# A sigmoid-attention and token-mixing kernel: every transpose in 64x64 tiles, PSUM as four pairs of banks, and a rewritten order

## The chip, the cores and the metric

The kernel runs on one core of a Trainium2 chip. The metric is the device time of one execution in microseconds (us), lower is better. The kernel before was timed three times: 203.85, 204.28 and 204.39 us, median 204.28 us.

Engine names in what follows are those of the profile: PE is TensorE's matmuls, PEld its weight loads, DVE is VectorE, ACT is ScalarE, POOL is GpSimd, SP is SyncE, which here only issues DMAs.

## The reference

Two stages, with batch B = 8, H = 12 heads, S = 448 tokens, head size 64, model size D = 768:

```python
scores = q @ k^T / sqrt(64) - log(S)          # per batch and head: 448 x 448
attn   = 1 / (1 + exp(-scores))               # a sigmoid, no softmax
x      = attn @ v, heads side by side         # (8, 448, 768)

wq, wk = x @ w_q, x @ w_k                     # (8, 448, 64) each
W_tok  = wq @ wk^T / sqrt(64)                 # token by token, per batch
mixed  = W_tok @ x
out    = max(mixed, 0) @ w_out                # (8, 448, 768), float32
```

Inputs and output are float32. Both kernels compute in bfloat16 with float32 accumulation.

## The kernel before, in words

Four heads of one batch are a **quad**; there are 24 quads, three to a batch. A quad's q, k and v arrive as one DMA each (`load1`, 448 KB), POOL casts them to bfloat16 (`cast1`), PE transposes q and k (`tr`), and DVE copies the transposes from PSUM to SBUF. For quads 16 to 22 (`TWICE`) q and k take another way: four DMAs load them in an overlapping layout (216 KB each, so 864 KB in place of 448 KB), POOL casts them into pairs, and DVE's own transpose (L154) does the work that PE does for the others.

The work is named by letters, and one string, `PLAN`, is the order written out by hand in which they are issued. PE runs its instructions in that order:

- `S` (`scores`): one seventh of a quad's scores, four 64x64-tile matmuls of 448 columns, one in each quarter of the array; then one ACT sigmoid of 128 x 896 into `at`. There are 168 of them, seven to each line of `PLAN`.
- `P` (`values`): one seventh of attn @ v, four 64x64-tile matmuls of 448 columns, accumulated over seven; after the seventh a DVE copy to `xt`.
- `q`, `k` (`tr`): seven transposes on the whole 128x128 array, then a DVE copy. `K` is a rest of the first quad's k.
- `x` (`tr_x`): eight 128x128 transposes of `xt`, DVE copy to `xn`.
- `W`, `N`, `U`, `M` (`mlp_wqk`, `mlp_wkn`, `mlp_tmp`, `mlp_mix`): the token mixing of one batch. `W` is a 128x128 matmul of 448 columns, `N` four 128x128 transposes, `U` eight 128x64-tile matmuls of 384 columns, `M` four 64x64-tile matmuls of 448 columns and a relu.
- `O` (`out_chunk`): a 128 x 384 piece of the output, six 128x128 matmuls of 384 columns, then a copy to SBUF and, for every second one, two DMAs to the output. In `U`, `M` and `O` a small letter puts the copy on ACT, a capital on DVE.

So PE works in three ways of splitting its array: 64x64 (`S`, `P`, `M`), 128x128 (`q`, `k`, `x`, `W`, `N`, `O`) and 128x64 (`U`).

PSUM has eight banks. Three pairs (`free2`) serve `S`, `P` and `M`; two single banks (`free1`) serve all other steps. A step takes the bank that has been free longest, so the order of release decides which reader a step waits for.

Loads are issued on SP in the order of the list `ORDER`, each as soon as its buffer is free (`pump_loads`); the casts run on POOL in the same order (`pump`). The last line of `PLAN` has no `S` left: its steps, with the last output pieces, are the tail, where copies are shared out between DVE and ACT and half of the stores are issued from ACT.

Of the kernel before, what the change touches and what calls it, by code (L numbers as in the profile page):

```python
# [16 lines left out]
def kernel(  # L17
# [36 lines left out]
    p_lb = pool("lb", 2)  # L54
# [10 lines left out]
    ps_f = pool("ps_f", 1, space=bass.MemoryType.PSUM)  # L65

    free2 = ["a", "b", "c"]
    free1 = ["d", "e"]

    def bank2(name):  # L70
        n = free2.pop(0)
        return n, ps_q.tile([P, 2, 512], F32, tag=n, name=name)

    def bank(shape, dtype, name):
        n = free1.pop(0)
        return n, ps_f.tile(shape, dtype, tag=n, name=name)
# [23 lines left out]


    TWICE = {'q': (16, 17, 18, 19, 20, 21, 22), 'k': (16, 17, 18, 19, 20, 21, 22)}

# [3 lines left out]
    def load1(n, nm, eng):  # L107
        u, j = quads[n]
        if n in TWICE.get(nm, ()):
            t = p_lb.tile([P, 2, 14 * HD], F32, tag=nm + "b32", name=nm + "b32")  # L110
            for g in range(2):
                src = SRC[nm][u, 4 * j + 2 * g : 4 * j + 2 * g + 2].rearrange(
                    "h (p r) d -> p h (r d)", r=14
                )
                for dh in range(2):
                    r0 = 64 * g + 32 * dh
                    eng.dma_start(  # L117
                        out=t[r0 : r0 + 32, :, 0 : 13 * HD + 32],
                        in_=src[:, :, 32 * dh : 32 * dh + 13 * HD + 32],
                    )  # L120
        else:
            t = p_ld.tile([P, 2, NI * HD], F32, tag=nm + "32", name=nm + "32")
            eng.dma_start(  # L123
                out=t,
                in_=SRC[nm][u, 4 * j : 4 * j + 4].rearrange(
                    "(g h) (p i) d -> (h p) g (i d)", g=2, i=NI
                ),
            )
        ld[nm, n] = t

    def cast1(n, nm, eng):
        if n in TWICE.get(nm, ()):
            t16 = p_c16.tile([P, 2, NI, 32, 2], BF16, tag=nm + "16", name=nm + "16")
            eng.tensor_copy(  # L134
                out=t16.rearrange("p h i d y -> p h y i d"),
                in_=ld.pop((nm, n)).rearrange("p h (y i d) -> p h y i d", y=2, d=HD)[..., 0:32],
            )
        else:
            p = p_v16 if nm == "v" else p_c16
            t16 = p.tile([P, NI, 2, HD], BF16, tag=nm + "16", name=nm + "16")  # L140
            eng.tensor_copy(  # L141
                out=t16.rearrange("p i b d -> p b i d"),
                in_=ld.pop((nm, n)).rearrange("p b (i d) -> p b i d", i=NI),
            )
        ld[nm + "16", n] = t16

    qk = {}

    def tr(n, nm):
        t16 = ld.pop((nm + "16", n))  # L150
        t = p_qk.tile([P, 2, NI, NP], BF16, tag=nm + "t", name=nm + "t")
        qk[nm, n] = t
        if n in TWICE.get(nm, ()):
            nc.vector.transpose(  # L154
                out=t.rearrange("p h i n -> p (h i n)").bitcast(F32),
                in_=t16.rearrange("p h i d y -> p (h i d y)").bitcast(F32),
            )
            return
        fb, ps = bank([P, NI, 2, NP], BF16, "pt" + nm)
        for i in range(NI):  # L160
            nc.tensor.transpose(  # L161
                ps[:, i].rearrange("p h n -> p (h n)"),
                t16[:, i].rearrange("p b d -> p (b d)"), ident16,
            )
        nc.vector.tensor_copy(out=t, in_=ps.rearrange("p i h n -> p h i n"))  # L165
        free1.append(fb)
# [3 lines left out]
    def scores(n, i):  # L170
        fb, sc = bank2("sc")
        for g in range(2):
            for h in range(2):
                nc.tensor.matmul(  # L174
                    sc[HALF[h], g, 0:S], qk["k", n][HALF[g], h, i, :],
                    qk["q", n][HALF[g], h].rearrange("p i n -> p (i n)"), start=True, stop=True,
                )
        at = p_at.tile([P, 2, S], BF16, tag="at", name="at")
        nc.scalar.activation(at, sc[:, :, 0:S], ACTF.Sigmoid, bias=bias_t, scale=attn_scale)  # L179
        free2.append(fb)  # L180
        ats[n, i] = at
# [3 lines left out]
    def values(n, i, tail):  # L185
        u, j = quads[n]
        if i == 0:
            pv[n] = bank2("pv")
        fb, ps = pv[n]
# [6 lines left out]
        if i == NI - 1:  # L196
# [5 lines left out]
            free2.append(fb)  # L202
# [3 lines left out]
    def tr_x(n, tail):  # L206
        u, j = quads[n]
        if j == 0:
            xns[u] = p_x.tile([P, 4, D], BF16, tag="xn", name="xn")
        fb, ps = bank([P, 4, 2, 2, HD], BF16, "px")  # L210
        for h in range(2):
            for m in range(4):
                nc.tensor.transpose(  # L213
                    ps[:, m, :, h], xt(u, j)[:, h, m * P : (m + 1) * P], ident16
                )
        for g in range(2) if tail else (slice(0, 2),):
            w = slice(2 * j * P, 2 * (j + 1) * P) if not tail else slice((2 * j + g) * P, (2 * j + g + 1) * P)
            COPY["s" if tail and g else "v"](  # L218
                out=xns[u][:, :, w],
                in_=ps[:, :, g].rearrange("p m h d -> p m (h d)")  # L220
                if tail else ps.rearrange("p m g h d -> p m (g h d)"),
            )
        free1.append(fb)
# [4 lines left out]
    def mlp_wqk(u, c, tail):  # L228
        if c == 0:
            pw[u] = bank([P, S], F32, "pw")  # L230
        fb, ps = pw[u]
# [3 lines left out]
        if c == NC - 1:  # L235
# [6 lines left out]
            free1.append(fb)  # L242

    def mlp_wkn(u):
        fb, ps = bank([P, 4, P], BF16, "pk")
        for m in range(4):
            nc.tensor.transpose(ps[:, m], wqks[u % 2][:, m * P : (m + 1) * P], ident16)
        wkn[u] = p_one.tile([P, 4, DH], BF16, tag="wkn", name="wkn")
        nc.vector.tensor_copy(out=wkn[u], in_=ps[:, :, 64:128])
        free1.append(fb)  # L250

    def mlp_tmp(u, act):
        tmps[u] = p_one.tile([P, NB], BF16, tag="tmp", name="tmp")
        fb, ps = bank([P, NB], F32, "pt")
# [7 lines left out]
        free1.append(fb)  # L262
# [7 lines left out]
    def mlp_mix(u, c, act, tail):  # L270
        if c == 0 and u % 2 == 0:
            mxs[u // 2] = [p_mx.tile([P, 2, 2, S], BF16, tag=f"mx{n}", name="mx") for n in range(NC // 2)]
        fb, ps = bank2("pm")
# [13 lines left out]
        free2.append(fb)  # L287
# [3 lines left out]

    def out_chunk(act, tail):
        w, m, nb = chunks.pop(0)
        if nb == 0:
# [3 lines left out]
        def block(ps, w0, w1):  # L298
            for c in range(NC):
# [14 lines left out]
        fb, ps = bank([P, NB], F32, "po")  # L314
        if tail and w == NU // 2 - 1 and not chunks:
            h = NB // 2
            block(ps[:, 0:h], NB, NB + h)
            nc.vector.tensor_copy(out=o[:, NB : NB + h], in_=ps[:, 0:h])
            fb2, ps2 = bank2("po")
            block(ps2[:, 0, 0:h], NB + h, D)  # L320
            nc.scalar.copy(out=o[:, NB + h :], in_=ps2[:, 0, 0:h])
            store(slice(NB, NB + h))
            store(slice(NB + h, D))
            return
        block(ps, nb * NB, (nb + 1) * NB)
        COPY["s" if act else "v"](out=o[:, nb * NB : (nb + 1) * NB], in_=ps)  # L326
        free1.append(fb)
# [39 lines left out]
    fb, ps = bank2("pwarm")  # L367
    for _ in range(32):
        nc.tensor.matmul(ps[:, 0, 0:P], zeros, zeros, start=True, stop=True)
    free2.append(fb)  # L370
    for t in xts:
        nc.vector.memset(t[:, :, S:], 0.0)
    for t in wqks:
# [4 lines left out]
        "v0 q1 k1 v1 k2 q2 q3 k3 q4 k4 v2 k5 k6 w0 k7 v3 "  # L378
        "w1 q5 q6 k8 v4 w2 q7 w3 v5 w4 k9 q8 v6 q9 w5 w6 "
        "v7 q10 k10 v8 v9 q11 k11 q12 v10 k12 v11 q13 k13 k14 q14 q15 "  # L380
        "v12 q16 k15 v13 v14 q17 k16 v15 k17 q18 k18 q19 v16 k19 v17 k20 "
        "k21 v18 v19 v20 v21 q20 q21 q22 v22 q23 k22 k23 v23 "
# [3 lines left out]
    BACK = {}  # L386
    for nm in "qkv":
        mine = {True: [], False: []}
        for n in range(N):
            kind = n in TWICE.get(nm, ())  # L390
            BACK[nm, n] = (kind, list(mine[kind]))
            mine[kind].append(n)

    def pump_loads():
        while len(loaded) < len(ORDER):
# [5 lines left out]
            else:  # L401
                kind, before = BACK[nm, n]
                back = 2 if kind else 3
                if len(before) >= back and (nm, before[-back]) not in cast:
# [35 lines left out]
    for nm in "qk":  # L440
        qk[nm, 0] = p_qk.tile([P, 2, NI, NP], BF16, tag=nm + "t", name=nm + "t")

    def tr_part(nm, t16, r, e, b=None):
        shape = [P, r.stop - r.start, 2, NP]
        fb, ps = (None, ps_q.tile(shape, BF16, tag=b, name="pt" + nm)) if b else bank(shape, BF16, "pt" + nm)
        for i in range(r.start, r.stop):
            nc.tensor.transpose(
                ps[:, i - r.start].rearrange("p h n -> p (h n)"),
                t16[:, i].rearrange("p b d -> p (b d)"), ident16,
            )  # L450
        COPY[e](out=qk[nm, 0][:, :, r], in_=ps.rearrange("p i h n -> p h i n"))  # L451
        if fb:
            free1.append(fb)
# [3 lines left out]
    tr_part("k", k016, KA, "v", free2[-1])  # L457
# [7 lines left out]
        "SSSKSPPSqPSkSPPP",  # L465
        "SSqPSkSqSPkSqSPPPP",
        "SkSPPSxSSkPPPPSxSk",
# [90 lines left out]
```

## Time and profile before

| what | value |
|---|---|
| median of 3 runs | 204.28 us (203.85 to 204.39) |
| the profiled execution | 204.95 us, of which the span of the program is 203.2 us |
| PE busy | 192.2 us (95%), 2388 matmuls |
| ACT busy | 171.2 us (84%) |
| DVE busy | 123.1 us (61%) |
| POOL busy | 80.3 us (40%) |
| read from HBM, written | 41.75 MB, 11.01 MB |
| TensorE clock granted, mean | 0.992 |
| first `S` matmul, last sigmoid's end, end of the span | 6.38, 177.69, 203.2 us |

A busy PE is not PE at its peak: a matmul's row lasts longer than the time after which the next one may start. Where one row of the chain of waits follows the other on PE without a gap, the rows' lengths are what a step costs. The profiled execution was 0.67 us above the median, and 1.75 us of it lies outside the span.

### The profile page before, as it was taken

The page shows a single profiled execution, that of the slowest core. Times are in us where ns is not written, and L with a number is a line of the kernel's source. Part 1 is how long each engine was busy: PE and PEld are TensorE (multiplying, and loading weights), DVE is VectorE, ACT ScalarE, POOL GpSimd, SP SyncE. Part 2 cuts the span into 40 slices and gives each one's busy share as a digit, 9 for nine tenths or more (in the row PEclk, how much of TensorE's full clock was granted, in tenths as well). Part 3 has the DMA queues.
Part 4 walks back from the last instruction along what each step waited for, and adds up shares of the span by engine and source line. Part 5 has one row for each costly group of instructions (what it writes and reads, how often), then busy time and mean ns, then how long its engine had stood idle before and what let it go on. Part 6 is the DMA issues. An engine that isn't in the chain of part 4 may idle for free.

```text
span 203.2 us, 5863 instructions
## 1 busy us (share of the span) xinstructions
PE 192.2 (95%) x2388; PEld 108.6 (53%) x2388; DVE 123.1 (61%) x196; ACT 171.2 (84%) x200; POOL 80.3 (40%) x95
## 2 busy tenths in 40 slices
PE   7669999999999999999999999999999899999991
PEld 7335545545556566555656555545455455555561
DVE  2226655866498567668777776858777654471230
ACT  4796999999989999889999999898998959974511
POOL 1577688676416624217642442511632600000000
PEclk9996999999999999999999999999999999999999
DMA  6999999899998999999999999999899933303575
GB/s 193 374 383 375 325 380 355 245 395 382 380 381 258 331 254 317 223 265 261 247 223 285 256 282 236 367 260 252 258 287 214 345 90 78 80 3 97 152 203 168
DMA packets 27786, 53.13 MB, mean 262 GB/s; under 512 B 4464, under 2 KB 19952, under 8 KB 27760
## 3 DMA queue, kind: packets, MB, share of 16 engines
q1 hardware_dynamic: 26960, 51.19, 85.9%
q10 hardware_dynamic: 800, 1.57, 2.1%
q8 instruction: 18, 0.29, 0.6%
q14 instruction: 8, 0.07, 0.1%
HBM read 41.75 MB, written 11.01 MB: 260 GB/s over the span
## 4 chain that ended last, share of the span: by engine, by line
DMA 41%; PE 31%; SPq 8%; ACT 8%; issue 4%; POOL 4%; DVE 1%; ACTq 1%; POOLq 0%
DMA qb<-in_q_dram 17%; DMA kb<-in_k_dram 12%; PE po L300 11%; PE sc L174 6%; ACT at L179 6%; SPq L117 5%; PE pv L192 5%; DMA q<-in_q_dram 4%; DMA out_dram<-o 4%; DMA v<-in_v_dram 4%; SPq L123 2%; PE pw L232 2%; PE ptk L161 2%; POOL k L134 2%; PE pt L257 2%
## 5 line engine op out<-in xcount | busy, mean ns | idle before, releaser
L179 ACT ACTIVATE at<-sc,bias_t 128x896 bf16<-128x896 f32 x168 | 156.1, 1016 | 13.6 <-PE sc L174 12.7
L300 PE MATMUL po<-wout,mx 128*128 128x384 bf16 (+1 forms) x342 | 61.8, 324 | 0.5 <-ACT o L326 0.3
L174 PE MATMUL sc<-qt,kt 64*64 64x448 bf16 x672 | 57.3, 363 | 2.4 <-DVE kt L451 1.0
L192 PE MATMUL pv<-at,v 64*64 64x448 bf16 x672 | 43.2, 353 | 0.7 <-POOL v L141 0.6
L300 PEld LDWEIGHTS <-mx 128*128 128x128 bf16 x342 | 30.9, 98 | 24.0 <-issue 7.0
L174 PEld LDWEIGHTS <-kt 64*64 64x64 bf16 x672 | 22.1, 104 | 24.3 <-issue 13.0
L201 DVE CAST xt<-pv 128x896 bf16<-128x896 f32 x23 | 25.0, 1088 | 16.1 <-PE pv L192 15.9
L326 DVE COPY o<-po 128x384 f32<-128x384 f32 x39 | 21.7, 556 | 16.9 <-PE po L300 11.8
L141 POOL CAST v<-v 128x896 bf16<-128x896 f32 x24 | 22.4, 934 | 15.2 <-PE pv L192 7.8
L268 DVE TENSOR_SCALAR mx<-pm 128x896 bf16<-128x896 f32 (+1 forms) x24 | 23.0, 969 | 7.2 <-PE pm L277 7.1
L192 PEld LDWEIGHTS <-v 64*64 64x64 bf16 x672 | 20.2, 107 | 12.3 <-issue 2.0
L218 DVE COPY xn<-px 128x1024 bf16<-128x1024 bf16 (+1 forms) x24 | 15.9, 663 | 7.3 <-PE px L213 7.2
L141 POOL CAST q<-q 128x896 bf16<-128x896 f32 x16 | 14.9, 933 | 9.9 <-DMA out_dram<-o 4.4
L141 POOL CAST k<-k 128x896 bf16<-128x896 f32 x16 | 14.9, 933 | 7.1 <-DMA k<-in_k_dram 4.3
L134 POOL CAST k<-kb 128x896 bf16<-128x896 f32 x7 | 8.3, 1192 | 19.4 <-DMA kb<-in_k_dram 9.2
L134 POOL CAST q<-qb 128x896 bf16<-128x896 f32 x7 | 8.2, 1190 | 18.3 <-issue 7.9
L213 PE MATMUL px<-ident,xt 128*128 128x128 bf16 x192 | 14.8, 220 | 0.1
L326 ACT COPY o<-po 128x384 f32<-128x384 f32 x16 | 7.7, 482 | 8.1 <-PE po L300 8.0
L213 PEld LDWEIGHTS <-xt 128*128 128x128 bf16 x192 | 11.5, 98 | 5.6 <-issue 4.8
L165 DVE COPY qt<-ptq 128x896 bf16<-128x896 bf16 x16 | 9.7, 618 | 7.1 <-PE ptq L161 7.0
L232 PE MATMUL pw<-xt,wqk 128*128 128x448 bf16 x48 | 13.8, 356 | 0.0
L165 DVE COPY kt<-ptk 128x896 bf16<-128x896 bf16 x16 | 9.9, 619 | 5.7 <-PE ptk L161 5.5
(53 smaller groups left out, 125.6 us busy)
## 6 DMA issues: line engine op xcount, KB each, us to landing
v<-in_v_dram SPq DMA_DIRECT2D x24, 448.0 KB, 7.8
out_dram<-o SPq DMA_DIRECT2D x47, 192.0 KB, 6.0
q<-in_q_dram SPq DMA_DIRECT2D x17, 448.0 KB, 7.5
k<-in_k_dram SPq DMA_DIRECT2D x16, 448.0 KB, 8.5
qb<-in_q_dram SPq DMA_DIRECT2D x28, 216.0 KB, 6.9
kb<-in_k_dram SPq DMA_DIRECT2D x28, 216.0 KB, 7.4
w<-in_moe_w_out_dram SPq DMA_DIRECT2D x6, 384.0 KB, 7.5
out_dram<-o ACTq DMA_DIRECT2D x7, 192.0 KB, 3.2
```

What stands on the lines that cost most here:

```text
L134: eng.tensor_copy(out=t16.rearrange("p h i d y -> p h y i d"), in_=ld.pop((nm, n)).rearrange("p h (y i d) -> p h y i d", y=2, d=HD)[..., 0 ...
L141: eng.tensor_copy(out=t16.rearrange("p i b d -> p b i d"), in_=ld.pop((nm, n)).rearrange("p b (i d) -> p b i d", i=NI),)
L165: nc.vector.tensor_copy(out=t, in_=ps.rearrange("p i h n -> p h i n"))
L174: nc.tensor.matmul(sc[HALF[h], g, 0:S], qk["k", n][HALF[g], h, i, :], qk["q", n][HALF[g], h].rearrange("p i n -> p (i n)"), start=True, st ...
L179: nc.scalar.activation(at, sc[:, :, 0:S], ACTF.Sigmoid, bias=bias_t, scale=attn_scale)
L192: nc.tensor.matmul(ps[HALF[g], h, 0:S], ld["v16", n][HALF[h], i, g, :], ats[n, i][HALF[h], g, :], start=(i == 0), stop=(i == NI - 1),)
L201: nc.vector.tensor_copy(out=xt(u, j)[:, :, 0:S], in_=ps[:, :, 0:S])
L213: nc.tensor.transpose(ps[:, m, :, h], xt(u, j)[:, h, m * P : (m + 1) * P], ident16)
L232: nc.tensor.matmul(ps, wqk16[:, c, :], xt(u, c // 2)[:, c % 2, 0:S], start=(c == 0), stop=(c == NC - 1),)
L268: nc.vector.tensor_scalar(dst, ps, moe_scale, 0.0, ALU.mult, ALU.max)
L300: nc.tensor.matmul(ps, mxs[w][c % 3][:, c // 3].rearrange("p b s -> p (b s)")[:, m * P : (m + 1) * P], wout16[:, c, w0:w1], start=(c == 0) ...
L326: COPY["s" if act else "v"](out=o[:, nb * NB : (nb + 1) * NB], in_=ps)
```

## The change

- **Transposes.** `q`, `k`, `x` and `N` are made of 64x64 transposes, one in each quarter of the array: 28 for a `q` or a `k` (7 before), 32 for an `x` (8 before), 8 for an `N` (4 before). q's and k's transposes of a quad share a pair of banks, and one DVE copy of 128 x 1792 takes both out after k.
- **No loading twice.** `TWICE`, its DMAs, its casts and DVE's transposes are gone: quads 16 to 22 are loaded and transposed on PE like all others.
- **PSUM.** Four pairs, which any step may take; `W`, `N`, `U` and `O` take half a pair. There is one list, `free2`, and one of half-used pairs, `halves`.
- **Output pieces in halves.** An `O` is three matmuls in place of six, and `PLAN` has 112 of them in place of 56; the copy follows the second half, and other steps may stand between the two.
- **Fillers.** `F`, 16 matmuls of zeros (64x64 tiles, 128 columns) whose result nobody reads: 19 of them, all in the first three lines of `PLAN`.
- **Order.** `PLAN` and `ORDER` are new. In `PLAN` a `k` always stands after its `q`; in `ORDER` the second quad's q and k now come ahead of the first quad's v.

On PE the program grows from 4778 rows (matmuls and weight loads) to 8814.

```diff
+    pairs = [ps_q.tile([P, 2, 512], F32, tag=f"pp{n}", name=f"pp{n}") for n in range(4)]
+    free2 = [0, 1, 2, 3]
+    halves = []
...
-    TWICE = {'q': (16, 17, 18, 19, 20, 21, 22), 'k': (16, 17, 18, 19, 20, 21, 22)}
...
+    def transposes(ps, t16, r):
+        for x, i in enumerate(range(r.start, r.stop)):
             for g in range(2):
+                for h in range(2):
+                    nc.tensor.transpose(
+                        ps[HALF[g], h, x * NP : (x + 1) * NP], t16[HALF[h], i, g, :],
+                        ident16[HALF[h], HALF[h]],
                     )
...
     def tr(n, nm):
+        t = "qk".index(nm)
+        if t == 0:
+            ps_qk[n] = bank2()
+        fb, _, ps = ps_qk[n]
+        transposes(ps[:, :, t * S : (t + 1) * S], ld.pop((nm + "16", n)), slice(0, NI))
+        if t == 1:
+            qk[n] = p_qk.tile([P, 2, 2, NI, NP], BF16, tag="qk", name="qk")
+            nc.vector.tensor_copy(
+                out=qk[n].rearrange("p t h i n -> p t h (i n)"),
+                in_=ps[:, :, 0 : 2 * S].rearrange("p h (t x) -> p t h x", t=2),
             )
...
     def tr_x(n, tail):
+        fb, _, ps = bank2()
+        for m in range(4):
+            for h in range(2):
+                for g in range(2):
+                    for c in range(2):
+                        nc.tensor.transpose(
+                            ps[HALF[c], g, (2 * m + h) * HD : (2 * m + h + 1) * HD],
+                            xt(u, j)[HALF[g], h, (2 * m + c) * HD : (2 * m + c + 1) * HD],
+                            ident16[HALF[g], HALF[g]],
+                        )
...
     def out_chunk(act, tail):
+        if opened:
+            w, m, nb, fb, ps = opened.pop()
+            part = 1
+        else:
+            w, m, nb = chunks.pop(0)
+            fb, ps, _ = bank1()
+            part = 0
...
+        block(ps, nb * NB, (nb + 1) * NB, part * NC // 2, (part + 1) * NC // 2)
+        if not part:
+            opened.append((w, m, nb, fb, ps))
+            return
...
     ORDER = (
-        "v0 q1 k1 v1 k2 q2 q3 k3 q4 k4 v2 k5 k6 w0 k7 v3 "
...
+        "q1 k1 v0 q2 v1 q3 k2 k3 k4 q4 v2 k5 q5 k6 q6 w0 "
...
     PLAN = (
-        "SSSKSPPSqPSkSPPP",
-        "SSqPSkSqSPkSqSPPPP",
-        "SkSPPSxSSkPPPPSxSk",
...
-        "SqkPSPPPPPSPSNOSSxkS",
...
-        "PPPPPmPPWxWWWWWxmMNouoooMmMoOooOoOOooO",
+        "FFSSSFFFFKFFSSFFFFqSkPPPSPPP",
+        "SSFFFFPSqSkxSPSPqkSPF",
+        "SPSPPPSqkFSqkSxFSPSPqk",
...
+        "SqkSoOSMSoOSqkPSPPPSPPP",
...
+        "PPPPPPmPMOoWWooOoxNxOOOuOomMmooooOOOoOOoOooooooO",
     )
```

## The prediction

> **What bounds the kernel now.** I read the page's first two parts, then the chain of waits in windows, then busy time by windows. First the busy totals and the slices:
>
> ```profile
> PE 192.2 (95%) x2388; PEld 108.6 (53%) x2388; DVE 123.1 (61%) x196; ACT 171.2 (84%) x200; POOL 80.3 (40%) x95
> ...
> ACT  4796999999989999889999999898998959974511
> ...
> PEclk9996999999999999999999999999999999999999
> DMA  6999999899998999999999999999899933303575
> ```
>
> PE is busy nearly throughout, but ACT is too in the first third, and the DMA engines are until slice 32. Which of them ends last? Busy time by windows (columns: length, then busy us and instructions of PE, PEld, DVE, ACT, POOL, then the granted clock, DMA share and GB/s):
>
> ```profile
> 6.40:20.00 13.60, 10.46 (x130) 5.37 (x130) 4.51 (x8) 11.30 (x12) 9.70 (x11) 0.87 1.05 380
> 20.00:54.00 34.00, 33.62 (x474) 18.41 (x474) 22.38 (x32) 33.42 (x38) 25.70 (x31) 1.00 1.01 351
> 54.00:177.70 123.70, 122.76 (x1600) 68.79 (x1593) 86.03 (x127) 113.19 (x126) 43.49 (x46) 1.00 0.93 254
> 177.70:203.20 25.50, 20.45 (x162) 11.66 (x154) 8.11 (x16) 10.70 (x22) 0.00 (x0) 1.00 0.47 124
> ```
>
> From 20 to 54 us ACT has 0.6 us of idle time in 34; from 54 us to the last sigmoid it has 10.5 idle and PE 0.9. So ACT sets the pace first, PE later; the tail is a matter of its own. ACT's pace is in its timeline, seven sigmoids without a gap:
>
> ```profile
> 23.84 6.41 ACT L179 ACTIVATE at<-sc,bias_t 128x896 bf16<-128x896 f32 x7
> ```
>
> The last of them lasts about 1.07, so the pitch is (6.41 - 1.07)/6 = 0.89 us. PE's prices are in the chain (start, us, what, matmuls), where PE follows PE:
>
> ```profile
> 50.99 0.45 PE px L213 x8
> 51.43 0.50 PE sc L174 x8
> 51.94 1.08 PE po L300 x6
> ...
> 53.24 0.31 PE sc L174 x4
> 53.55 0.95 PE pv L192 x20
> 54.50 0.19 PE sc L174 x4
> 54.69 0.77 PE pt L257 x8
> ```
>
> Five `P` cost 0.95, so a 64x64-tile group of four with 448 columns costs 0.188. A 128x128 transpose costs 0.0556 (px, 0.45 for eight). An `S` costs 0.19 where it has one neighbour of its own tiling after it and 0.31 where it borders on another: a change of tiling costs 0.12. Six `O` matmuls cost 0.97 without it, `U` 0.64.
>
> DMA has a large share of the whole chain, but PE waited for a load visibly only once after 54 us, for a `kb` of the twice-loaded kind:
>
> ```profile
> 148.63 9.96 DMA kb<-in_k_dram
> ...
> 158.74 1.20 POOL k L134
> 159.96 0.65 DVE kt L154
> 160.61 0.52 DVE qt L165
> 161.17 0.55 PE ptk L161 x7
> ```
>
> Three `S` run on PE from 159.28 to 161.17, 1.89 in place of 0.69; the third of them waited for that `kt` of L154. Cost: about 1.2 us.
>
> **A ledger by lines of PLAN.** Lines 1 to 24 hold seven `S` each. For each I add PE's steps and changes of tiling, and ACT's 7 x 0.89 = 6.22 plus 0.5 for each output copy on ACT, and take the larger, since only two or three `S` fit into PSUM ahead of ACT. Before: PE 160.6, ACT 152.4, sum of the larger 165.7 (PE is larger in 15 lines). With the 6.4 us to the first `S` that gives 172.1; the last sigmoid ended at 177.7. So 5.6 us of waits are left: some 3 at the start, 1.2 for `kb`, the rest small. The tail took 25.5, with 20.7 of PE work.
>
> **The change, part by part.**
>
> *Transposes.* The trace has no 64-column matmul. By columns, a group of four costs 64/448 x 0.188 = 0.027; the 128-column transpose lies 0.002 above its own columns' 0.0536, so 0.029. That makes `q` or `k` 7 x 0.029 = 0.205 (0.39 before), `x` 0.235 (0.445), `N` 0.12 (0.22; two quarters only, four pairs). The upper end is the group at its present pace whatever its columns, 0.188, or 1.31 for a `q`. I take 0.029, because the 128-column row is the nearest in kind and size and shows next to no fixed cost; all four quarters start within one group in the `S` rows. Before: 32 q/k x 0.39 + 24 x 0.445 + 8 x 0.22 = 25.0. After: 46 x 0.205 + 24 x 0.235 + 8 x 0.12 = 16.0, although 14 transposes come over from DVE. PE: -9.0.
>
> *Changes of tiling.* Counted along the two PLANs: 170 before, 114 after, halves of `O` included. 56 x 0.12 = -6.7 on PE.
>
> *Fillers.* 19 x 4 groups x 128 columns = 19 x 0.22 = +4.1 on PE, all in lines 1 to 3, where PE then has 5.5, 4.2 and 4.3 against ACT's 6.22: ACT hides them. Without that cover they cost the 4.1. What they can give is the clock, 0.87 in the window from 6.4 to 20 us: 13% of 10.5 us of PE, at most 1.4. I take nothing.
>
> *No loading twice.* 14 x 416 KB less to read (6 of 41.75 MB), 42 fewer issues on SP, casts of 0.93 in place of 1.19. None of it is on PE's path but the 1.2 us at 160, which goes. What is late there next is ACT.
>
> *Copies.* DVE: 14 transposes and 32 copies of 0.62 become 23 copies of 128x1792. From 0.36 us for 384 and 0.69 for 1024 columns in bfloat16 such a copy is some 1.1 us. DVE falls by about 3 us and is not the bound. k's copy now ends 0.5 later; the second quad's first `S` follows its `k` after one `S` and six `P`, 1.3 us, which covers it; the later quads have three or more sigmoids.
>
> *PSUM.* Following `free2` through both PLANs, an `S` gets the pair of the `S` two before it in 103 of 168 cases before and 110 after, and that of the `S` just before it 1 time before, 4 after. Each such case idles ACT for some 0.4 (the matmuls and the way to ACT). Other steps that must wait for a recent `S`'s sigmoid: 12 before, 28 after; there one more `S` is always queued for ACT, and behind the waiting PE stands work that ACT does not need yet. Price: 4 x 0.4 = 1.6 if nothing covers it, 0 if ACT has a backlog. I take 0 and keep 1.6 for the range.
>
> *Sum.* With these prices lines 1 to 24 give PE 150.4, ACT 154.7 (more output copies sit on ACT), sum of the larger 162.5. As an example line 12, `SqkPPSPPPSPPSOOSqkSoOSPPx`: 16 x 0.188 + 4 x 0.205 + 0.235 + 4 x 0.485 + 5 x 0.12 = 6.6 against ACT's 6.22. So PE gives up 10 us, and only 3.2 of them show, as ACT is next. Last sigmoid: 6.4 + 162.5 + (5.6 - 1.2) = 173.3. Tail: PE 19.2 in place of 20.7, the rest of it as before: 24.0. Span 197.3, 5.9 less; the profiled execution would be 199.0 against 204.95. The median lies 0.67 below the profiled time: 198.3.
>
> **A rule against it.** The densest stretch is this window:
>
> ```profile
> 62.00:82.00 20.00, 20.00 (x297) 12.25 (x300) 13.15 (x20) 19.06 (x22) 10.11 (x13) 1.00 0.99 283
> ```
>
> That is 30 PE rows (matmuls and weight loads) per us; the changed program needs 8814 in some 185 us, 48 per us. No row shows that PE takes so many. The Trainium skill, "TensorE: Matmul & The Clock Gate", section "Wait — 56ns, not 53.3ns?", says that start-to-start of matmuls never falls below about 25 ns however few columns they have. Read as one floor for all four quarters together, a `q` would cost 0.70 and an `x` 0.80, the ledger would give 188.1, and the time about 225; read as a floor for each quarter it changes nothing. The `S` rows, with four matmuls in one 0.188 group, do not decide between the two.
>
> **Rivals.**
>
> 1. *PE cannot take the rows (slower).* The densest steady pattern shown is 8 rows per 0.188 group, 42.7 per us. Were that PE's limit, 8814 rows take 206 us; with the start and the 6.2 us from the last matmul to the end the time is about 218. It decides from 46 rows per us on down (8814 over 203.2 - 6.4 - 6.2). For it: nothing denser is in the trace. Against it: the 42.7 are explained by the columns alone. Chance 0.18.
> 2. *The weight load of a 64-column group is not hidden (slightly slower).* After a change of tiling a first group takes some 0.03 more (an `S` at 34.84 us is followed by a `P` at 35.06, 0.22 in place of 0.19), about the time of 64 columns. If every short group pays it, it costs 0.056 like a 128x128 transpose; the ledger gives 170.1, the tail 24.6, the time 206.5. It passes the time before at 0.049 per group. Against it: in `P` the loads cost nothing. Chance 0.14.
> 3. *Sharing PSUM starves ACT.* Transposes are cheap, but the 28 and 4 waits above, the pair held from `q` to `k` and halves held by open `O`s cost 0.2 us apiece; 200 to 206. Chance 0.10, half of it still faster.
> 4. *The forecast*, 192 to 203. Chance 0.58. Its low end: the waits at the start halve, and PE's surplus in the late lines (162.5 - 154.7 = 7.8) is half covered by earlier lines' slack.
>
> **The numbers.** 0.3% is about what a measurement of this kernel can tell from no change. Faster 0.58 + 0.05 = 0.63, within it 0.04, slower 0.33. The range goes from 192, the forecast's low end, to 212, past the second and third rival and into the first; what it leaves out is most of the first rival and a little below, 0.18.
>
> **What would show it.** Right: in the chain, `pp` of 28 matmuls at some 0.2 us, without 0.12 next to an `S`; ACT idle less than 6 us between the first and the last sigmoid, last sigmoid near 173; PE busy in fewer slices, with idle time released by ACT. Wrong: 28 transposes taking 0.4 (rival 2) or 0.7 and more (rival 1), ACT waiting for PE in every line; or ACT idle before `S` while PE waits for ACT or DVE to free a pair (rival 3).

## The result: 243.3 us in place of 204.3, and the profile after

The changed kernel took 243.26 us (median of 4 runs, 240.28 to 243.87), the kernel before, in the same series, 204.33 us (203.85 to 204.53): a ratio of 1.188 with a 95% interval of 1.178 to 1.198. The forecast was 198.3 and the range ended at 212. The profiled execution was 243.87 us with a span of 242.0; all sums below are made against that span and the 203.2 us of before. Some executions of a kernel are slower than its others, whatever the kernel: the times below are of the faster ones, but the profiles kept of b_qk64 and b_fill are of slower ones.

First the page, busy totals and slices, as shown of before:

```profile
PE 195.2 (81%) x4406; PEld 112.3 (46%) x4406; DVE 122.0 (50%) x170; ACT 174.0 (72%) x202; POOL 76.1 (31%) x95
...
ACT  4444853999586879697899976987696788846421
PEclk9995987899889999999999999999999999999999
DMA  6999897368998775179975832575220422223465
```

PE has gone from 95% busy to 81%, ACT from 84% to 72%: neither is the bound any more. The granted clock, at 0.6 in one slice before, now dips in several of the first dozen. By windows:

```profile
6.40:20.00 13.60, 5.77 (x280) 4.41 (x274) 1.39 (x2) 5.61 (x6) 7.96 (x9) 0.89 1.04 372
20.00:54.00 34.00, 24.89 (x791) 15.90 (x782) 13.81 (x17) 24.34 (x26) 17.58 (x22) 0.84 0.76 246
54.00:216.30 162.30, 140.55 (x3062) 76.31 (x3062) 96.62 (x123) 131.84 (x146) 49.16 (x57) 0.99 0.58 182
216.30:242.00 25.70, 18.76 (x202) 10.83 (x201) 8.10 (x16) 9.61 (x20) 0.00 (x0) 1.00 0.47 123
```

The last row ends the same as before: the tail is 25.7 us against 25.5. Everything is lost ahead of the last sigmoid, which ends at 216.3 in place of 177.7. From 6.4 to 20 us PE is busy for 5.77 us of 13.6 (10.46 before) and ACT for 5.61 (11.30 before), and the losses thin out later. What PE does there is in its timeline (start, us, what, matmuls, and in brackets the idle time before and what ended it):

```profile
59.99 0.35 PE L211 MATMUL pp<-ident,xt 64*64 64x64 bf16 x21
63.13 0.28 PE L211 MATMUL pp<-ident,xt 64*64 64x64 bf16 x11 [2.79 <-issue]
63.23 0.38 PE L170 MATMUL pp<-qk 64*64 64x448 bf16 x4
63.42 0.41 PE L145 MATMUL pp<-ident,q 64*64 64x64 bf16 x28
63.64 0.38 PE L188 MATMUL pp<-at,v 64*64 64x448 bf16 x4
...
66.66 0.65 PE L170 MATMUL pp<-qk 64*64 64x448 bf16 x4
67.04 0.65 PE L188 MATMUL pp<-at,v 64*64 64x448 bf16 x4
```

Three things are to be read here. The `q` of 28 transposes starts at 63.42 and the next step at 63.64: 0.22 us, so the short transposes are as cheap as forecast. But PE stops for 2.8 us in the middle of one `x`, after 21 of its 32 transposes, and the release is "issue": the instruction that follows waits for nothing that the profile shows. And shortly after, an `S` takes 0.38 (66.66 to 67.04) where it takes 0.19 elsewhere: PE runs at half its clock.

The view of waits has twelve such stops (us in total, times, longest), where PE has none in the kernel before:

```profile
PE pp L145 <- issue: 10.7, 6, 4.4
PE pp L506 <- issue: 7.3, 2, 3.9
PE pp L211 <- issue: 3.4, 2, 2.8
PE pp L188 <- issue: 1.5, 2, 1.0
```

From here on a stop or a wait is counted from the time at which the matmul ahead would have let the next one start, which is mostly 0.1 to 0.3 us longer than the idle time that a view gives. Counting PE's rows from the program's start shows where these stops lie. All of those that I count, 13 with 25.2 us in all (the twelve, and one too short for the view), stand at a row number that leaves 191 when divided by 256:

```
row at which PE stops   at us     stop, us   the steps there
 447                      8.45     3.6       filler | filler
 703                     14.00     4.6       k | k
1215                     27.25     1.0       k | k
1471                     31.23     2.6       k | k
1727                     36.43     4.1       filler | filler
2751                     60.15     3.0       x | x
3775                     85.90     1.7       q | q
4799                    110.47     1.3       k | k
(5 others, 3.4 us in all: rows 2239, 3263, 3519, 4031, 7359)
```

256 rows are one packet of the instruction queue (packets, MB, share of 16 engines): its 34 packets carry 16 KB each, and 8814 rows are 34.4 times 256. Before, there were 18 packets for 4778 rows, 18.7 times 256.

```profile
q8 instruction: 34, 0.56, 1.0%
```

and of before:

```profile
q8 instruction: 18, 0.29, 0.6%
```

The trace gives the start of each such packet, so a block of 256 rows can be followed: when PE begins it, when the packet for the next block starts, when PE gets on with that next block.

```
kernel    block    PE begins   next packet   PE begins     length   late by   packet
                   it          starts        next block                       to use
before      447     23.12       26.16         32.55          9.4     3.0       6.4
before     3775    150.00      154.50        159.49          9.5     4.5       5.0
after       447     12.11       16.04         18.58          6.5     3.9       2.55
after      1471     33.88       38.22         40.63          6.7     4.3       2.41
after      2495     57.19       60.68         63.13          5.9     3.5       2.45
```

While the loads run, a packet starts only some time after PE has entered the block ahead of it, and where PE stops it goes on 2.2 to 2.8 us after the packet's start. In the kernel before the same lateness stood under blocks of 8 to 12 us, and a packet started 5 to 11 us ahead of its use; no such stop is to be seen there. With blocks that PE could do in 4 us it is in the open.

The second group of new stops have a wait. PE waits 26.9 us on semaphores in the changed kernel and 9.9 before, and the largest of the new ones stand in the later part, where the fetch is no longer in the way (timeline of after):

```profile
95.66 0.36 PE L235 MATMUL pp<-xt,wqk 128*128 128x448 bf16 x1
95.86 0.65 PE L318 MATMUL pp<-wout,mx 128*128 128x384 bf16 x3
97.26 0.35 PE L235 MATMUL pp<-xt,wqk 128*128 128x448 bf16 x1 [0.74 <-ACT o L348]
...
98.73 0.35 PE L235 MATMUL pp<-xt,wqk 128*128 128x448 bf16 x1
99.87 0.65 PE L318 MATMUL pp<-wout,mx 128*128 128x384 bf16 x3 [0.78 <-DVE wqk L240]
```

A `W` (L235) that goes on accumulating in its half of a pair waits for the copy of the `O` (L318) that was issued just ahead of it, which sits in the other half; and an `O` waits for the copy of a `W`. Neither needs the other's data: the pair is one allocation, and the wait is set for all of it. I count ten waits of a `W` behind an `O` (9.2 us), four of an `O` behind a `W` (3.8), four of an `O` behind a `U` (2.8) and one of an `O` behind an `N` (1.1): 17 us, all new.

The sum: PE's columns at full clock fell from 161.3 to 155.2 us and its changes of tiling from 171 to 115, at 0.12 each, so PE gave up 12.8. The fetch adds 25.2 and the waits 17.0. The clock was at half for 17 us ahead of the last matmul, 3.4 before; the columns that PE ran in them are worth 7.4 us at full clock against 1.4, so half the clock cost about 5.9 more. Other short stops add some 1.2. That is -12.8 + 25.2 + 17.0 + 5.9 + 1.2 = 36.5 of the 38.8 us that the span grew.

### The profile page after: what moved, and what is told of

It reads as the page before. It is cut to its first block, busy times and chain, and to the rows that moved or that the text cites. A ratio compares the mean times of both kernels' runs of the same rounds, so it can differ in the third digit from the quotient of the medians.

```text
span 242.0 us, 9858 instructions
## 1 busy us (share of the span) xinstructions
PE 195.2 (81%) x4406; PEld 112.3 (46%) x4406; DVE 122.0 (50%) x170; ACT 174.0 (72%) x202; POOL 76.1 (31%) x95
## 3 DMA queue, kind: packets, MB, share of 16 engines
HBM read 35.78 MB, written 11.01 MB: 193 GB/s over the span
## 4 chain that ended last, share of the span: by engine, by line
PE 67%; issue 13%; DVE 8%; ACT 7%; DMA 3%; ACTq 1%; DVEq 0%
PE pp L318 21%; PE pp L170 15%; PE pp L188 14%; PE pp L145 6%; ACT at L175 5%; PE pp L235 3%; PE pp L211 3%; PE pp L506 2%; PE pp L266 2%; DVE mx L277 2%; PE pp L286 2%; DMA q<-in_q_dram 1%; DVE o L348 1%; DVE wqk L240 1%; ACT o L348 1%
## 5 line engine op out<-in xcount | busy, mean ns | idle before, releaser
L175 ACT ACTIVATE at<-pp,bias_t 128x896 bf16<-128x896 f32 x168 | 157.9, 1009 | 48.6 <-PE pp L170 47.7
L318 PE MATMUL pp<-wout,mx 128*128 128x384 bf16 (+1 forms) x342 | 64.3, 324 | 7.4 <-DVE wqk L240 3.4
L170 PE MATMUL pp<-qk 64*64 64x448 bf16 x672 | 65.1, 375 | 1.0 <-ACT at L175 0.5
L188 PE MATMUL pp<-at,v 64*64 64x448 bf16 x672 | 49.3, 370 | 2.5 <-issue 1.5
L318 PEld LDWEIGHTS <-mx 128*128 128x128 bf16 x342 | 30.5, 97 | 35.6 <-issue 19.5
L158 DVE COPY qk<-pp 128x1792 bf16<-128x1792 bf16 x23 | 25.1, 1091 | 32.2 <-PE pp L145 32.1
L170 PEld LDWEIGHTS <-qk 64*64 64x64 bf16 x672 | 24.5, 110 | 27.1 <-issue 22.4
L197 DVE CAST xt<-pp 128x896 bf16<-128x896 f32 x23 | 25.1, 1090 | 20.1 <-PE pp L188 18.0
L131 POOL CAST v<-v 128x896 bf16<-128x896 f32 x24 | 22.4, 934 | 40.5 <-PE pp L188 39.8
L348 DVE COPY o<-pp 128x384 f32<-128x384 f32 x38 | 21.2, 558 | 22.2 <-PE pp L318 19.9
L277 DVE TENSOR_SCALAR mx<-pp 128x896 bf16<-128x896 f32 (+1 forms) x23 | 22.6, 988 | 13.2 <-PE pp L286 12.5
L235 PE MATMUL pp<-xt,wqk 128*128 128x448 bf16 x48 | 14.6, 354 | 7.7 <-DVE o L348 4.0
L224 DVE COPY xn<-pp 128x1024 bf16<-128x1024 bf16 (+1 forms) x24 | 15.9, 666 | 9.0 <-PE pp L211 8.9
```

The source lines that it names most:

```text
L131: eng.tensor_copy(out=t16.rearrange("p i b d -> p b i d"), in_=ld.pop((nm, n)).rearrange("p b (i d) -> p b i d", i=NI),)
L158: nc.vector.tensor_copy(out=qk[n].rearrange("p t h i n -> p t h (i n)"), in_=ps[:, :, 0 : 2 * S].rearrange("p h (t x) -> p t h x", t=2),)
L170: nc.tensor.matmul(sc[HALF[h], g, 0:S], qk[n][HALF[g], 1, h, i, :], qk[n][HALF[g], 0, h].rearrange("p i n -> p (i n)"), start=True, stop=True,
L188: nc.tensor.matmul(ps[HALF[g], h, 0:S], ld["v16", n][HALF[h], i, g, :], ats[n, i][HALF[h], g, :], start=(i == 0), stop=(i == NI - 1),)
L197: nc.vector.tensor_copy(out=xt(u, j)[:, :, 0:S], in_=ps[:, :, 0:S])
L235: nc.tensor.matmul(ps, wqk16[:, c, :], xt(u, c // 2)[:, c % 2, 0:S], start=(c == 0), stop=(c == NC - 1),)
```

## The experiments

The first theory, the fetch theory or A in the texts, is that PE runs out of instructions at the ends of blocks, and that loads make it worse. The rival is that waits for PSUM, from pairs shared by all steps, set the end; the texts call it, together with the short transposes, theory B, and its part on `W` and `O` theory C. Whether the 64x64 transposes are to blame in themselves is asked of the kernel before.

### More rows in the kernel before (b_cut4)

Only the rows are added: before's order, its banks and its transposes stay.

```diff
-                    sc[HALF[h], g, 0:S], qk["k", n][HALF[g], h, i, :],
-                    qk["q", n][HALF[g], h].rearrange("p i n -> p (i n)"), start=True, stop=True,
...
+        for z in range(4):
...
+                    w = slice(112 * z, 112 * (z + 1))
...
+                        sc[HALF[h], g, w], qk["k", n][HALF[g], h, i, :],
+                        qk["q", n][HALF[g], h].rearrange("p i n -> p (i n)")[:, w], start=True, stop=True,
```

> The kernel before, with each matmul of an S cut into four of 112 columns: the same columns on PE, the same order, PSUM, loads and copies, but 8810 PE rows in place of 4778 (the changed kernel has 8814). Theory A (PE runs out of instructions: a block of 256 rows cannot be fetched faster than every 5 to 6.5 us while the loads fill the DMA queues): stalls of 1 to 4 us without a wait every 256 rows, some of them followed by a halved clock, 222 to 242 us. Theory B (the loss of the changed kernel comes from the short transposes or from sharing PSUM, not from the number of rows): 203 to 208 us.

Measured: 233.42 us (231.78 and 235.06), 1.138 times before, 1.119 to 1.157. Its timeline has the same stop in the middle of a step, and its view of waits the sum of them for scores (us in total, times, longest):

```profile
86.27 0.68 PE L176 MATMUL sc<-qt,kt 64*64 64x112 bf16 x39 [2.95 <-issue]
```

```profile
PE sc L176 <- issue: 19.2, 12, 3.0
```

The stops add up to 23.8 us, and all stand at rows that leave 191 by 256; waits on semaphores are 11.4 us, 1.5 more than before. With the columns unchanged, rows alone cost 28 us against the kernel before in the same series (205.15). This is the strongest evidence for the fetch: no short transpose, no shared pair and no filler is in this kernel.

### Light loads in the changed kernel (a_light)

```diff
     def load1
...
-            out=t,
+            out=t[:, :, 0:HD],
...
-            ),
+            )[:, :, 0:HD],
...
     def cast1
...
-            in_=ld.pop((nm, n)).rearrange("p b (i d) -> p b i d", i=NI),
+            in_=ld.pop((nm, n))[:, :, None, 0:HD].to_broadcast([P, 2, NI, HD]),
```

> The changed kernel with the loads of q, k and v cut to the first of seven rows of each partition (64 KB in place of 448 KB; the cast spreads that row over the tile, so the result is another), all else the same, 8814 PE rows. Theory A, as fetching queues behind the loads: the fetch of a block starts within 1 us of the block before (now 1 to 4 us), the stalls without a wait shrink from 25 us to under 6 and the halved clock goes, 208 to 218 us, the waits between W and O staying. Theory A2 (a fetch takes its 5 us whatever else the DMA engines do): 235 us or more. Theory B: no change from 243 but by the earlier loads, 238 or more.

Measured: 221.57 us (221.17 and 221.98), 21.7 less than the changed kernel with the same instructions on PE. Stops for instructions fell from 25.2 to 7.9 us, and the clock stayed at full speed (windows of this kernel, as of the others):

```profile
6.40:20.00 13.60, 10.18 (x503) 7.55 (x493) 4.30 (x5) 11.72 (x13) 9.85 (x12) 1.00 0.39 85
```

In this stretch PE does 10.18 us of work in place of 5.77 and ACT 11.72 in place of 5.61, with 85 GB/s of loads in place of 372. The blocks tell why: in this kernel's first 30 us the packets start 1.0 to 1.7 us after PE enters a block, not 1.2 to 4.3, while from the packet's start to its use it still takes 2.3 to 2.8 us where PE stops. So a block that ends in a stop lasts 3.5 to 4.3 us here (60 to 74 rows per us), and mostly 5.4 to 6.7 us under the full loads (38 to 48 rows per us; three of twelve took 4.0 to 4.7). The late start is what the loads cost. PE's waits on semaphores stayed at 26.9 us, so they are another matter. The time is above the 208 to 218 us that theory A gave, and the stops above its 6 us; the packets start later than within the 1 us that it expected.

### The changed kernel with 128x128 transposes (a_128)

```diff
-        transposes(ps[:, :, t * S : (t + 1) * S], ld.pop((nm + "16", n)), slice(0, NI))
+        t16 = ld.pop((nm + "16", n))
+        for i in range(NI):
+            nc.tensor.transpose(
+                ps[:, t, i * P : (i + 1) * P], t16[:, i].rearrange("p b d -> p (b d)"), ident16,
+            )
```

(`x` and `N` in the same way; 5666 rows.)

> The changed kernel with q, k, x and N transposed on the whole 128x128 array again (5666 PE rows in place of 8814), the order, the four pairs, the halves and the fillers staying. Theory A: hardly a stall without a wait is left, 25 us of them and some 6 us of halved clock go, 9 us of transposes and some 60 changes of tiling (7 us) come back: 222 to 232 us. Theory B (PSUM sharing alone makes the loss): 255 us or more, since PE's work grows by 16 us.

Measured: 236.24 us (235.92 and 236.56). The fetch stops shrink to two, 4.2 us, both at the start beside the fillers, but PE's columns return (170.2 us) and so do changes of tiling (207), which together are 26 us more than in the changed kernel. Waits are 22.4 us. So 21 us of fetch were exchanged for 26 us of PE, while some 5.5 us of low clock and 4.5 of waits went. The gain of 7 us is smaller than I expected, because the short transposes do save what was forecast.

### A whole pair for W (a_wpair)

```diff
-            pw[u] = bank1()
+            pw[u] = bank2()
```

> The changed kernel with W taking a whole pair of banks, so that it never shares a pair with an O. Theory C (a W or O waits for the copy out of the other half of its pair, 14 us in the trace where one follows the other): these waits of 0.8 to 1.1 us go, the stalls without a wait stay: 227 to 234 us. If the waits are for true reuse of banks: 240 to 247 us, as fewer banks are left for the rest.

Measured: 243.93 us (243.14 and 244.73): nothing gained. The waits of a `W` behind an `O` are gone, and other steps wait for one of the now scarcer pairs:

```profile
PE pp L318 <- ACT at L175: 6.8, 14, 0.7
```

This kind of wait is not among the changed kernel's longer ones; PE's waits are 28.1 us in all. The wait changes its owner when the number of pairs stays at four. Fetch stops are no more than in the changed kernel, but 27 us are at half clock in place of 17, so the two times do not compare the waits alone.

### Three pairs and two single banks in the changed kernel (a_32)

```diff
-    pairs = [ps_q.tile([P, 2, 512], F32, tag=f"pp{n}", name=f"pp{n}") for n in range(4)]
+    pairs = [ps_q.tile([P, 2, 512], F32, tag=f"pp{n}", name=f"pp{n}") for n in range(3)]
+    ones = [ps_q.tile([P, 512], F32, tag=f"pq{n}", name=f"pq{n}") for n in range(2)]
```

(`bank1` takes a single bank, or a whole pair where none is free.)

> The changed kernel with PSUM as before: three pairs, and two single banks of their own for W, N, U and O in place of half pairs; order, transposes, fillers and rows (8814) as changed. Theory C (an open W waits for the copy of an O that only shares its pair): the waits of W after O and of O after W, 14 us, go, the stalls without a wait stay at 20 to 27 us: 228 to 236 us unless the three pairs make S wait more. If the wait is for true reuse: 242 us or more.

Measured: 246.12 us (246.05 and 246.20). The neighbours' waits are gone, since single banks have no neighbour, and an `S` now waits for a pair:

```profile
PE pp L167 <- ACT at L172: 7.8, 18, 0.7
```

Waits on semaphores are 36.9 us, 10 more than in the changed kernel, and fetch stops 16.1, 9 less, since the blocks are stretched by the waits; 27 us are at half clock. The new order was written for four pairs; the split of before doesn't fit it.

### Short transposes in the kernel before (b_x64, b_qk64, b_all64)

```diff
-        fb, ps = bank([P, 4, 2, 2, HD], BF16, "px")
+        fb = free2.pop(0)
+        ps = ps_q.tile([P, 2, 1024], BF16, tag=fb, name="px")
...
+                            ps[HALF[c], g, (2 * m + h) * HD : (2 * m + h + 1) * HD],
+                            xt(u, j)[HALF[g], h, (2 * m + c) * HD : (2 * m + c + 1) * HD],
+                            ident16[HALF[g], HALF[g]],
```

In b_x64 that is done for `x`, and `N` is cut in four as well; b_qk64 does it for `q` and `k`; b_all64 for all. Since a transpose of one row half writes into a bank of its own, as in the changed kernel, each such step takes a pair.

> One part of the change alone: the kernel before, with only x and N in 64x64 transposes (x takes a pair of the three in place of a single bank), 5994 PE rows. The short transposes themselves are cheap on the trace of the changed kernel (28 in 0.22 us), so PE falls by 24 x 0.21 + 8 x 0.1 and 6 changes of tiling, 6.5 us, of which ACT's pace lets 2 to 4 show. Theory A: at 30 rows per us a block of 256 rows lasts 8 us, longer than a fetch, so hardly a stall without a wait is added: 199 to 203 us. Theory B (the short transposes are what is slow, or pairs in place of single banks): 206 us or more.

> One part of the change alone: the kernel before, with only q and k (those that are not loaded twice) in 64x64 transposes, each in a pair of banks, 6122 PE rows. PE falls by 32 x 0.17 and some 35 changes of tiling, 9 to 10 us, of which ACT's pace lets 3 to 5 show. Theory A: most of the added rows stand in the first two thirds, where loads fill the DMA queues; a block lasts 7 us there, so a few stalls of up to 1 us: 199 to 204 us. Theory B: 206 us or more.

> The kernel before with q, k, x and N in 64x64 transposes, its order, its three pairs and two single banks and its twice-loaded quads staying, 7338 PE rows. PE falls by some 16 us. Theory A: 37 rows per us on average, a block lasts 7 us and less than 6 where transposes crowd, near the limit: 5 to 12 us of stalls without a wait eat the gain, 200 to 212 us, between the parts and the kernel with cut matmuls. Theory B: 210 us or more, the sum of the two parts' losses.

Measured: b_x64 214.73 us, 1.053 times before (1.047 to 1.059); b_qk64 218.36 us and b_all64 228.39 us (one execution each), where the kernel before took about 204. I had expected a gain from the first two. Fetch stops are 0.1 us in b_x64 and 1.7 in b_all64 (5994 and 7338 rows), and PE's columns did fall, to 154.9 and 148.9 us. What came in their place are waits for pairs, 25.3 us and 44.9 where before had 9.9. In b_x64:

```profile
64.88 0.56 PE L161 MATMUL ptq<-ident,q 128*128 128x128 bf16 x7
65.74 0.45 PE L216 MATMUL px<-ident,xt 64*64 64x64 bf16 x32 [0.29 <-ACT at L179]
```

The `x` waits for a sigmoid to give up a pair, which it never did when it had a single bank, and everything behind it on PE waits with it. So the short transposes need twice the banks for a time, and with three pairs this costs more than the columns bring: -6.4 us of columns against +15.4 of waits.

### W ahead of O (a_swap, a_swap_light)

```diff
-        "SPPPSPPSOWOSMSWoWMSWoWSM",
+        "SPPPSPPSWOOSMSWWoMSWWoSM",
...
-        "SPSWoWOSxSWOOWSMSOOWSqk",
+        "SPSWWoOSxSWWOOSMSWOOSqk",
```

(twelve lines of `PLAN` in this way)

> The changed kernel with one edit of PLAN: in 12 lines, a W that stands directly behind an O changes places with it, so that no W opens its half of a pair right after an O whose copy is still to come. 8814 rows as in the changed kernel; all else alike. Theory C (a W behind an O waits for the copy of its pair's neighbour, about ten times 0.8 to 1.0 us): these waits go, the 25 us of instruction fetch stay where the blocks of 256 rows end, so 230 to 236 us. Rival (the fetch sets the end and the waits lie within time that PE has over before the next block): no gain, 241 to 245 us.

> The kernel with the light loads (q, k and v read 64 KB of their 448 KB and the casts repeat them, so that the rest of the inputs is not read) with the swapped W and O as well. The light loads alone took 221.6 us. If the two losses add, the waits of W behind O (some 9 us) go here too: 211 to 214 us, fetch stalls about 8 us. If the swap only shifts the waits to others, 219 to 223 us.

Measured: a_swap 237.0 us (235.8 and 238.2), 6.3 less than the changed kernel; a_swap_light 213.55 us (213.17 and 213.93), 8.0 less than a_light. PE's waits fell from 26.9 to 19.5 and from 26.9 to 17.9 us, and the lines of after's timeline shown above read here:

```profile
93.93 0.55 PE L235 MATMUL pp<-xt,wqk 128*128 128x448 bf16 x2
94.32 0.65 PE L318 MATMUL pp<-wout,mx 128*128 128x384 bf16 x3
94.90 0.38 PE L170 MATMUL pp<-qk 64*64 64x448 bf16 x4
```

Two `W`, one after the other, then the `O`, and no idle time. With full loads one part of the gain is lost again (fetch stops 22.7 in place of 25.2, but 24 us at half clock in place of 17), so it is 1 us short of what I gave it; with light loads it is whole. The two causes add up: light loads take off 21.7, the swap 6.3, both 29.7, a little more than their sum of 28.0. What stays above the kernel before in a_swap_light, 8.1 us of span, is 8.3 of fetch and 8.0 more of waits less 12.8 of PE and some 1.4 of clock; these make 2.1, so about 6 us are not accounted for.

### Without fillers (a_noF)

```diff
         if t == "F":
-            for _ in range(4):
-                for g in range(2):
-                    for h in range(2):
-                        nc.tensor.matmul(
-                            pairs[free2[0]][HALF[h], g, 0:P], zeros[HALF[g], 0:64], zeros[HALF[g], :],
-                            start=True, stop=True,
-                        )
```

> The changed kernel without its 19 fillers F; 8206 rows in place of 8814. Fetch theory: the rows of the first three lines are fewer, so the stalls that lie in the first 40 us (3.6, 4.6, 2.6 and 4.1 us) shrink by a third to two thirds, and the whole is 5 to 10 us shorter: 233 to 239 us. Rival: the fillers keep the clock up and ACT sets the pace there anyway, so without them the low clock costs what the fetch gives: 242 us or more.

Measured: 239.64 us (239.48 and 239.80), 3.6 less by the medians, but the fastest of the changed kernel's four executions took 240.28: the fillers cost somewhere between nothing and their columns (4.1), not more. Fetch stops fell by 9.2 us, to 16.0, all at rows that again leave 191 by 256 although every step has moved by up to 608 rows, so the place belongs to the row number and not to a step. But waits rose to 34.7 us and the time at half clock to 27. The time lies just outside the expected 233 to 239, between theory and rival.

### Two groups of fillers in the kernel before (b_fill)

```diff
-        "k21 v18 v19 v20 v21 q20 q21 q22 v22 q23 k22 k23 v23 "
+        "k21 v18 v19 v20 v21 q20 q21 q22 k22 v22 q23 k23 v23 "
...
-        "SSqPSkSqSPkSqSPPPP",
+        "SSFqPSkFSqSPkSqSPPPP",
```

(`F` is 20 matmuls of zeros, 128x128 with 128 columns, into a single bank.)

> The kernel before with two groups of 20 filler matmuls (128x128, 128 columns, zeros) in the second line of PLAN in place of the 16 fillers it issues inside each of its first steps, and with the loads of k22 put ahead of v22 and q23; 4858 rows. Meant to keep what the changed kernel aimed at and leave out what cost it. Theory: rows stay far below 40 per us, so no fetch stall; the 3.4 us at half clock after 16.3 us go (up to 1.5 us) and so does the wait for kb near 159 us (up to 1.2 us): 201 to 204 us. Rival: ACT sets the pace where the clock was low, and the wait was covered by a later one: 204 to 205 us, no difference that can be measured. A third: the fillers hold a bank that another step needs: 205 to 207 us.

The fillers are only added here; the kernel before has none in its first steps, and the text is wrong on that. Measured: 1.0037 times before, 1.0003 to 1.0071, so no gain, and between nothing and 1.4 us lost. From its profile I read the kinds of waits, and the clock of the first stretch:

```profile
6.40:20.00 13.60, 12.02 (x151) 7.04 (x143) 3.83 (x6) 9.89 (x11) 9.64 (x11) 0.75 1.05 379
```

```profile
DVE o L326 <- DMA out_dram<-o: 11.0, 5, 2.8
PE po L300 <- DVE o L326: 3.2, 3, 1.5
```

PE is busier from 6.4 to 20 us, but the granted clock is 0.75, not 0.87. Over the nine executions behind the ratio the mean granted clock is 0.980 to 1.000, and 0.982 to 1.000 in the kernel before: the fillers did not raise it. In this profile the wait for `kb` is gone and another has come: DVE's copies wait for output stores to land (3.3 us before), and an `O` on PE waits for DVE. Whether the load moved ahead on SP is what delays the stores was not tested. No version here beats the kernel before.

## Why the prediction failed, point by point

**Transposes, tiling, loads: held.** A `q` of 28 takes 0.22 (forecast 0.205), an `x` 0.25 between neighbours at 113.86 and 114.11 us (0.235). Changes of tiling are 115 (114), and 35.78 MB are read in place of 41.75. PE gave up 12.8 us against a forecast of -9.0 - 6.7 + 4.1 = -11.6. The tail kept nothing of it: PE's busy time there fell from 20.45 to 18.76 us, but it took 25.7 us, not 24.0, with waits of 1.4, 0.7 and 0.5 us on PE. The reading of 25 ns as one floor for all four quarters, 0.70 for a `q`, is refuted by the 0.22; with 0.031 per group of four, a floor for each quarter is neither reached nor refuted.

**The step that failed first: "A rule against it" and rival 1.** Rows per us were the right question, and the limit was put in the wrong place. I asked how fast PE can start rows, and took 42.7 per us as the densest steady pattern; the transposes above run at 28 x 2 rows in 0.22 us, some 250 per us. The limit is how fast rows arrive. It has no single rate: mostly 38 to 48 rows per us under full loads, 60 to 74 under light ones, and it bites where a block of 256 dense rows comes, above all while the queues are full: 11 of the 13 stops and 23 of their 25 us lie in the first 92 us. Rival 1's point of decision, 46 rows per us on down, was met there, though by another limit than the one it names, and more than its 0.18 could have been given to it: the view of DMA queues has the instruction queue with its 18 packets, and 8814 rows against 4778 would have said that PE needs a packet every 5 to 6 us. The packets' lateness was in the trace of before too (0.1 to 4.5 us), hidden under blocks of 8 to 12 us. The Trainium skill has the blocks: "Runtime: NRT & Kernel Launch", section "Instruction fetch mechanics", says that instructions are refilled in blocks of 16 KiB, 256 instructions, and that crossing a boundary is mostly hidden. The 256 rows are what the trace shows; "mostly hidden" holds for the kernel before and not for this one, with up to 4.6 us at a boundary.

**"ACT hides them": failed.** The fillers were to lie in PE's spare time in lines 1 to 3. Two of the stops (3.6 and 4.1 us) are in the midst of fillers: a filler of 32 rows is an eighth of a block, so it brings the next boundary nearer. Without them the kernel is 3.6 us faster by the medians, which is about the spread of its executions.

**PSUM, "I take 0 and keep 1.6": failed.** I followed `free2` for `S` alone, where little happened. The price lay with steps that share a pair: rival 3 names the halves held by open `O`s and prices them at 0.2 us, but the waits are 0.6 to 1.4 us, since the copy of a neighbour has to be done whole, and there are 19 of them on PE: 17 us. That the swap of letters takes 6 to 8 us off shows it for `W` behind `O`; for `O` behind `W`, `U` and `N` it was only read from the trace.

**The clock, "I take nothing": failed in sign.** Fillers were to raise it, and the fetch stops lowered it. In the changed kernel half clock comes in stretches of 3.4 us or multiples, each beginning within or just after a stop of 2.6 us or more (the first stop, of 3.6, brought none), and it is gone in a_light, where no stop is over 1.8. That about 5.9 us are due to it is an estimate from the columns that ran in those stretches; no run took the clock alone away.

**The sum's frame.** The ledger took the larger of PE and ACT line by line, and added the old waits as a constant, 5.6 less 1.2. ACT's idle time ahead of sigmoids is 48.6 us where less than 6 was forecast, and 47.7 of it is released by PE's scores:

```profile
ACT at L175 <- PE pp L170: 47.7, 45, 5.0
PE pp L235 <- DVE o L348: 4.0, 6, 0.7
PE pp L235 <- ACT o L348: 3.6, 4, 1.3
```

A model of busy times can't see either of the new costs: one is a time in which PE waits for nothing that the profile names, the other depends on which neighbour a step gets.

## What to carry to other kernels

Cutting a step into more and shorter instructions has a price beside its busy time: count instructions per us for each stretch, and compare a block of 256 of them with the time that the profile shows between the starts of instruction packets and their use, loads running. Stops that are released by "issue" in the middle of a step, at a fixed distance in instructions, are the sign of it. And when banks are merged into one allocation so that any step may use them, look for steps that stay open there while a neighbour comes and goes: order them so that the one that stays open comes ahead of its neighbour, which took 6 to 8 us off here. Keeping its bank apart gained nothing while the number of banks stayed the same (a_wpair, a_32).

## What the runs showed of the hardware that I had not expected

- PE's instructions come in packets of 16 KB, 256 rows, about one block ahead: under loads, the packet for the next block starts after PE has entered the present one. It takes 0.9 to 1.6 us by its own record, and PE, where it has stopped, goes on 2.2 to 2.8 us after its start.
- These packets are delayed when the queues are full of loads: in the changed kernel's blocks that end in a stop they start 2.4 to 4.3 us after PE's entry into the block where 226 to 389 GB/s were moved in it and 1.2 to 1.3 us where it was 82 to 168; in the first 30 us of a_light 1.0 to 1.7 us, with 58 to 142 GB/s.
- The PE clock falls to half in units of 3.41 us. "TensorE: Matmul & The Clock Gate" of the Trainium skill, Part 1, gives the same unit and the same halving after an idle window; what is new here is that stops for instructions are followed by it, also some that are shorter than such a window: in b_cut4 one of 2.4 us, at 184.7 us, is followed by 3.4 us at half clock (others, of up to 3.1 us, are not).
- Four 64x64 transposes of 64 columns, one in each quarter of the array, take 0.031 us, or 0.0079 us apiece.
